# Folding a Fourier stage a second time, with padded rest rows and early small loads, in a sketched-attention and Fourier-mixing kernel

## Chip, cores and metric

One core of one Trainium2 chip at a time; kernels are compared by their ratios to the kernel before. The metric is device time in microseconds (us), median of several executions. Ratios of two kernels are computed as the mean time of one kernel's fast runs over the mean time of the other's fast runs of the same rounds, so they are not quite the ratio of the medians quoted. "State" is a label on a run: on one core a run is called slow when it lies over 1.5% above the fastest of the same kernel.

## The reference, cut to what matters

```python
# attention with quadratic sketch features, B=4, H=4, S=1088, D=32, r=8
phi(x)[i*8+j] = (S1 x)[i] * (S2 x)[j]                     # 64 features
kv = sum_s phi(k_s) v_s ;  z = sum_s phi(k_s)
x_s = phi(q_s) kv / (phi(q_s) z + 1e-6)                   # heads side by side: 128 columns
# Fourier mixing and an MLP on x [4, 1088, 128]
u  = x + real(fft(fft(x, axis=s), axis=d))
un = (u - mean) / sqrt(var + 1e-6)
out = u + relu(un @ w1) @ w2
```

The Fourier transform along s is computed as matmuls with cosine and sine tables. Because the input is real, only half of the output frequencies are computed; the other half are mirrored copies.

## The kernel before

`a` is the Fourier matmul stage for one batch and one table (i = 0 cosine, i = 1 sine). The sums x[s] + x[s+544] and x[s] - x[s+544] (even and odd frequencies) already halve the length: four chunks of 128 rows, and a rest of 64 rows, with two batches sharing one 128-row rest tile.

```python
def fold(self, t0):                      # POOL, once per half of a batch
    gpsimd.tensor_tensor(xp[:, t0:t0+2, :], xf[:, t0:t0+2, 0, :], xf[:, t0:t0+2, 1, :], ADD)
    gpsimd.tensor_tensor(xm[:, t0:t0+2, :], xf[:, t0:t0+2, 0, :], xf[:, t0:t0+2, 1, :], SUB)
    gpsimd.tensor_copy(xb[...], xf[...])         # bf16 copies of x, two
def a(self, i):
    b, tab = self.b, (ctab, stab)[i]
    r0 = 64 * (b % 2)
    bn, pz = self.pz[i] = ps(2, [[512, 2], [1, 512]])
    for par in range(2):
        xx = (xps, xms)[par][b]
        for t in range(4):
            nc.tensor.matmul(pz[:, par, 0:NK], xx[:, t, :], tab[:, t, par, :],      # NK = 273
                             start=(t == 0), stop=False)
        nc.tensor.matmul(pz[:, par, 0:NK], xrems[b // 2][r0 : r0 + 64, :],
                         tab[r0 : r0 + 64, 4, par, :], start=False, stop=True)
# ... (cut)
self.u_s = sb3.tile([128, 4, 128], FP32, name="us", tag="us")   # three buffers; stored from here
```

The program is emitted step by step from a list called ORDER, and each engine runs its own instructions in that order. The names: `wm1` a dummy matmul that wakes TensorE; `wt` transposes the sketches; `kT`, `qT` transposes of k, q on DVE; `pab` the features product of k; `tf` a step of the tables on DVE behind a POOL chain; `w1` centres the first MLP weight; `kv` the sum over k; `nd` the attention rows; `a` the Fourier stage; `us`, `st`, `mh`, `re`, `mm`, `ot` the MLP. Loads of batch 0 before: k on both queues, then the two small sketch loads, then the rest.

## Time and profile before

| | |
|---|---|
| time | 121.28 us median of 4 (120.54 to 121.82) |
| span of the profile | 119.8 us |
| first features product / first kv matmul | 11.4 / 19.4 us |
| Fourier stretch (first to last Fourier matmul) | 46.9 to 95.0 us: 48.1 us |
| after it, to the end | 24.8 us |

The three last rows are marks: the starts of the first and last matmul of a source line. They cut the span into start, middle and tail.

From the page of the kernel before: span; busy time, share and instruction count per engine; and PE busy in tenths over 40 slices of the span.

```profile
span 119.8 us, 3138 instructions
PE 105.2 (88%) x1191; PEld 70.3 (59%) x1191; DVE 79.8 (67%) x247; ACT 62.4 (52%) x148; POOL 42.0 (35%) x86
PE   6069998999999999999999999999999998966710
```

TensorE is full between the start and the tail, so work removed from it there should shorten the span until another engine takes over.

From the chain of waits of the kernel before (start, duration, what):

```profile
2.27 4.61 DMA s_68<-in_S_dram
...
7.28 4.38 PE pall L233 x10
...
47.06 0.47 PE pall L658 x4
47.52 0.22 PE pall L660
47.74 0.58 PE pall L658 x4
48.32 0.22 PE pall L660
...
103.51 3.34 DMA out_dram<-us
106.88 0.05 DVEq L558
106.97 0.70 DVE us L558
```

The sketch load is waited for and followed by ten dummies. In the Fourier stage, four full-height matmuls (L658) take 0.47 us, but the 64-row one (L660) takes 0.22 us, and the four after it take 0.58. In the tail, the chain goes through a store that is under way for 3.3 us before a copy into `us` can begin. That is not 3.3 us of idling: DVE had other work for most of it, and its waits list shows 1.2 us:

```profile
DVE us L558 <- DMA out_dram<-us: 1.2, 1, 1.2
```

From the waits of the weight loader before (line, waited for, us in total, times, longest):

```profile
PEld L660 <- issue: 3.4, 15, 0.2
```

Fifteen of the sixteen weight loads of the 64-row matmuls wait 0.23 us for nothing that the profile shows.

### The profile page before, as it was taken

The page shows a single profiled execution, that of the slowest core. Times are in us where ns is not written, and L with a number is a line of the kernel's source. Part 1 is how long each engine was busy: PE and PEld are TensorE (multiplying, and loading weights), DVE is VectorE, ACT ScalarE, POOL GpSimd, SP SyncE. Part 2 cuts the span into 40 slices and gives each one's busy share as a digit, 9 for nine tenths or more (in the row PEclk, how much of TensorE's full clock was granted, in tenths as well). Part 3 has the DMA queues.
Part 4 walks back from the last instruction along what each step waited for, and adds up shares of the span by engine and source line. Part 5 has one row for each costly group of instructions (what it writes and reads, how often), then busy time and mean ns, then how long its engine had stood idle before and what let it go on. Part 6 is the DMA issues. An engine that isn't in the chain of part 4 may idle for free.

```text
span 119.8 us, 3138 instructions
## 1 busy us (share of the span) xinstructions
PE 105.2 (88%) x1191; PEld 70.3 (59%) x1191; DVE 79.8 (67%) x247; ACT 62.4 (52%) x148; POOL 42.0 (35%) x86
## 2 busy tenths in 40 slices
PE   6069998999999999999999999999999998966710
...
GB/s 123 252 160 231 245 151 203 249 93 189 175 229 87 0 3 0 0 5 0 5 0 11 76 5 83 4 5 0 3 0 27 108 46 25 80 78 22 90 88 22
DMA packets 27967, 9.52 MB, mean 79 GB/s; under 512 B 20400, under 2 KB 26800, under 8 KB 27952
## 3 DMA queue, kind: packets, MB, share of 16 engines
...
q14 instruction: 6, 0.05, 0.1%
...
## 4 chain that ended last, share of the span: by engine, by line
PE 77%; DMA 7%; DVE 6%; ACT 3%; issue 2%; ACTq 1%; DVEq 0%
PE pall L405 13%; PE pall L493 13%; PE pall L458 8%; PE pall L331 8%; PE pall L658 7%; PE pall L614 5%; PE pall L233 4%; PE pall L595 4%; DMA s_68<-in_S_dram 4%; PE pall L660 3%; DMA out_dram<-us 3%; PE pall L680 3%; DVE stats L565 2%; DVE us L558 2%; PE pall L690 2%
## 5 line engine op out<-in xcount | busy, mean ns | idle before, releaser
L601 ACT ACTIVATE ht<-pall 128x512 bf16<-128x512 f32 (+1 forms) x36 | 18.2, 557 | 7.3 <-PE pall L595 7.2
L418 DVE TENSOR_TENSOR qpT<-pall,qa 128x1024 f32<-128x1024 f32 x8 | 9.7, 1214 | 10.7 <-PE pall L405 9.7
L614 PE MATMUL pall<-w_b,ht 128*128 128x128 bf16 x136 | 11.4, 220 | 2.0 <-ACT ht L601 0.9
L595 PE MATMUL pall<-uT,w_b 128*128 128x512 bf16 (+1 forms) x40 | 10.6, 347 | 1.8 <-ACT uT L587 1.0
L614 PEld LDWEIGHTS <-ht 128*128 128x128 bf16 x136 | 8.3, 97 | 6.4 <-ACT ht L601 2.2
L626 DVE SCALAR_TENSOR_TENSOR us<-pall,rstd,us 128x128 f32<-128x128 f32 x33 | 9.4, 345 | 1.8 <-PE pall L614 1.1
L413 ACT COPY qa<-pall 128x1024 f32<-128x1024 f32 x8 | 8.1, 1016 | 3.8 <-PE pall L405 3.6
L341 DVE TENSOR_TENSOR kp<-ka,pall 128x1024 f32<-128x1024 f32 x8 | 9.6, 1205 | 0.2 <-ACT ka L337 0.2
L331 PE MATMUL pall<-sblk,kT 128*128 128x128 f32 x64 | 9.4, 293 | 0.0
L331 PEld LDWEIGHTS pall<-sblk,kT 128*128 128x128 f32 x64 | 8.6, 206 | 0.8 <-issue 0.3
L565 DVE BATCH_NORM_STATS2 stats<-us 128x6 f32<-128x128 f32 x34 | 7.5, 280 | 1.8 <-ACT us L558 1.7
L405 PE MATMUL pall<-qT,wb 32*64 32x512 f32 x64 | 8.7, 610 | 0.0
L233 PE MATMUL pall<-wdummy 128*128 128x512 bf16 x18 | 7.5, 575 | 1.2 <-DVE wdummy L183 1.2
L405 PE MATMUL pall<-qT,wa 32*64 32x512 f32 x64 | 8.4, 606 | 0.0
L516 DVE TENSOR_TENSOR xf<-pall,rc 128x256 f32<-128x256 f32 x16 | 6.8, 425 | 0.7
L337 ACT COPY ka<-pall 128x128 f32<-128x128 f32 (+1 forms) x10 | 2.5, 249 | 8.1 <-PE pall L331 8.1
L510 DVE TENSOR_SCALAR rc<-pall 128x8 f32<-128x8 f32 (+1 forms) x20 | 3.2, 159 | 4.5 <-PE pall L493 3.4
...
L493 PEld LDWEIGHTS pall<-kvz_85,qpT 128*128 128x128 f32 x32 | 3.9, 191 | 2.5 <-issue 1.6
L558 ACT COPY us<-pall 128x512 f32<-128x512 f32 (+1 forms) x7 | 3.5, 494 | 3.2 <-PE pall L683 2.8
L298 POOL COPY cdc<-cd_192 128x128 bf16<-128x128 bf16 x1 | 0.3, 283 | 13.6 <-ACT cd_192 L296 13.6
L493 PEld LDWEIGHTS pall<-kvz_86,qpT 128*128 128x128 f32 x32 | 3.8, 192 | 1.9 <-issue 1.9
...
## 6 DMA issues: line engine op xcount, KB each, us to landing
...
```

The lines of the kernel that those rows point to most:

```text
L233: nc.tensor.matmul(w[:, :], wdummy[:, 0:128], wdummy[:, :], start=(i == 0), stop=(i == n - 1))
L331: nc.tensor.matmul(_v(self.ps, 0, 128, 32 * j, [[256, 2], [128, 2], [1, 32]]), lhsT, sblk2, start=True, stop=True, skip_group_check=True)
L341: nc.vector.tensor_tensor(out=_v(self.out, 0, 128, 0, [[64, n], [8, 8], [1, 8]]), in0=_v(self.ka, 0, 128, 0, [[8, n], [1, 8], [0, 8]]), in ...
L405: nc.tensor.matmul(pq[f0 : f0 + 64, g % 2, :], wt[32 * g : 32 * g + 32, :, :], self.qT[32 * g : 32 * g + 32, pr, 32:544], start=True, stop ...
L418: nc.vector.tensor_tensor(out=self.qpT[:, pr, :, 32:544], in0=pq, in1=self.qa[pr][:], op=MULT)
L458: nc.tensor.matmul(self.pkv[64 * h2 : 64 * h2 + 33, pr, :], lhsT, rhs, start=(j == 0 and pr == 0), stop=(j == 8), skip_group_check=True, t ...
L493: nc.tensor.matmul(pnd[:, 2 * a + pr, :], self.qpT[:, pr, a, 32 + 128 * c : 160 + 128 * c], kvz[:, pr, :], start=True, stop=True, skip_gro ...
L565: nc.vector.bn_stats(stats[:, i, :], self.u_s[:, i, :])
L595: nc.tensor.matmul(ph[:, 0:n], w1_b[:, 128 * cc : 128 * cc + 128], self.uT[:, 0:n], start=True, stop=True)
L601: nc.scalar.activation(out=self.ht[:, cc, 0:n], in_=ph[:, 0:n], func=ACT.Relu)
L614: nc.tensor.matmul(self.pm[:, i, :], self.ht[:, cc, 128 * i : 128 * i + 128], w2_b[:, cc, :], start=(cc == 0 and i == 0), stop=(cc == 3), ...
L626: nc.vector.scalar_tensor_tensor(out=ot[:, i, :], in0=self.pm[:, i, :], scalar=rstd[:, i : i + 1], in1=self.u_s[:, i, :], op0=MULT, op1=ADD)
```

## The change

The intent: x[s] and x[544-s] also share table rows up to a sign, so the folded rows can be folded once more, and two chunks do instead of four. For that, row 544-s must lie on the same partition as row s; the kernel gets it by writing half of the q feature columns reversed. The rest rows get a full 128-row tile per batch, padded with zeros. The sketch loads go first. In the same change come five buffers for `us`, a kv transpose done in two pieces, casts and reversals on other engines, 9 dummies instead of 18, and a new ORDER.

```diff
 def q_p(self, pr):
-    tensor_tensor(out=qpT[:, pr, :, 32:544], in0=pq, in1=qa, op=MULT)
+    tensor_tensor(out=qpT[:, pr, :, 32:288], in0=pq[:, :, 0:256], in1=qa[:, :, 0:256], op=MULT)
+    tensor_tensor(out=_v(qpT, 0, 128, 1088*pr + 543, [[544, 2], [-1, 256]]),
+                  in0=pq[:, :, 256:512], in1=qa[:, :, 256:512], op=MULT)
@@ fold
+def fold1(self, h, eng):      # f = x0 + x1, x0 - x1 (fp32)
+def fold2(self, h, eng):      # xc = sums and differences of the two halves of f (bf16)
@@ a
-    for t in range(4):
-        matmul(pz[:, par, 0:NK], xx[:, t, :], tab[:, t, par, :], ...)
-    matmul(pz[:, par, 0:NK], xrems[b // 2][r0:r0+64, :], tab[r0:r0+64, 4, par, :], ...)
+    combo = ((0, 3), (2, 1))[i][par]
+    for h in range(2):
+        matmul(pz[:, par, 0:NK], xcs[b][:, combo, h, :], tab[:, h, par, :], ...)
+    matmul(pz[:, par, 0:NK], xrems[b][:, :], tab[:, 2, par, :], ...)
@@ us
-    tile([128, 4, 128], FP32, name="us", tag="us")
+    tile([128, 4, 128], FP32, name="us", tag="us", bufs=5)
@@ loads of batch 0
+    the two sketch loads first on the ACT queue; q of batch 0 on the ACT queue, k head 2 on SP
 ... (cut: casts, kv transpose, reversals on DVE, ORDER)
```

More of the change, by code (lines that the diff above doesn't have):

```diff
@@ L28 @@
 ORDER = """
-wm1 wm1 wm1 wm1 wt wm1 wm1 wm1 wm1 wm1 wm1 wm1 wm1 wm1 wm1 kT0.1 wq qT0.1 qT0.0 kT0.0 pab0.1 w1 wm1
-pkr0 wm1 wm1 wm1 pab0.0 ka0.1 ka0.0 ktr0 tf0 kT1.0 kT1.1 kp0.1 tfd kp0.0 qT1.0 qA0.1 qA0.0 qB0.0
-qa0.0 qp0.0 pbr0 kv0.0 qB0.1 kar0 qa0.1 kv0.1 pab1.0 qC0 kpr0 qT1.1 qp0.1 kv0.2 ka1.0 kc0 pab1.1 kt0
-qc0 ka1.1 kz0 tf1 kp1.0 qd0 kT2.0 kp1.1 qA1.0 nd0.0 rc0.0 tf2 qa1.0 qB1.0 nd0.1 qB1.1 qA1.1 nd0.2
-qp1.0 ta1 qa1.1 tad ta0 kv1.0 kv1.1 nd0.4 nd0.3 kv1.2 pab2.0 rc0.1 qT2.1 qp1.1 rc0.2 rc0.3 fo0.1
@@ L34 @@
-fo0.0 kc1 ka2.0 kt1 kz1 qC1 ta2 qc1 qT2.0 rc0.4 kT2.1 tf3 tf4 nd1.0 qA2.1 qd1 kp2.0 rc1.0 qa2.1 ta3
-nd1.2 pab2.1 qA2.0 pkr1 qB2.1 qa2.0 ta4 qp2.1 rc1.2 nd1.1 nd1.3 a0.0 ka2.1 ktr1 z0.0 zr0.0 rc1.3
-rc1.1 kp2.1 a0.1 z0.1 zr0.1 fo1.0 fo1.1 qB2.0 kv2.0 pbr1 kv2.1 qC2 nd1.4 qp2.0 kT3.0 bb0.0 kar1
-us0.0 kpr1 rc1.4 st0.0 kv2.2 bb0.1 kc2 us0.1 st0.1 tt0.1 kt2 kz2 tt0.0 nd2.0 ut0.0 rs0.0 qc2 rc2.0
-mh0.0.0 nd2.1 mh0.0.1 mh0.0.2 re0.0.0 re0.0.2 re0.0.1 nd2.2 pab3.0 mh0.0.3 ud0.1 rc2.1 qT3.0 kT3.1
-qd2 ka3.0 re0.0.3 rs0.1 kp3.0 mh0.1.0 mm0.0.0 mm0.0.1 mm0.0.2 mm0.0.3 ot0.0 pab3.1 re0.1.0 mh0.1.3
@@ L40 @@
-mh0.1.1 re0.1.3 re0.1.1 nd2.3 rc2.2 rc2.3 qT3.1 fo2.0 mh0.1.2 qA3.0 mm0.1.0 qB3.0 mm0.1.1 re0.1.2
-qa3.0 ka3.1 mm0.1.2 mm0.1.3 qp3.0 kp3.1 ot0.1 qA3.1 a1.0 qC3 nd2.4 z1.0 qa3.1 zr1.0 a1.1 qc3 z1.1
-zr1.1 fo2.1 kv3.0 kv3.1 qB3.1 qp3.1 qd3 kv3.2 bb1.0 kc3 us1.0 tt1.0 kt3 bb1.1 kz3 st1.0 ud1.0 us1.1
-nd3.0 nd3.1 mh1.0.0 mh1.0.3 mh1.0.1 tt1.1 mh1.0.2 rc3.0 rc3.1 rc2.4 re1.0.0 re1.0.1 rs1.0 ut1.1
-re1.0.2 fo3.0 nd3.2 nd3.3 nd3.4 mm1.0.0 rc3.2 mh1.1.0 re1.0.3 re1.1.0 mh1.1.3 mh1.1.1 bbr0 re1.1.1
-rc3.3 st1.1 fo3.1 mh1.1.2 usr0 re1.1.3 re1.1.2 a2.0 mm1.0.1 mm1.1.0 mm1.1.1 mm1.1.2 mm1.1.3 ttr0
@@ L46 @@
-mm1.0.2 a2.1 mm1.0.3 rs1.1 z2.0 zr2.0 z2.1 str0 ot1.1 rc3.4 ot1.0 zr2.1 utr0 a3.0 mhr0.0 mhr0.1 a3.1
-mhr0.2 mhr0.3 z3.0 rsr0 rer0.0 z3.1 rdr0.3 rdr0.1 rer0.2 bb2.0 us2.0 st2.0 tt2.0 mmr0.0 mmr0.1
-mmr0.2 bb2.1 mmr0.3 zr3.1 zr3.0 otr0 uv2.1 st2.1 ut2.0 mh2.0.0 mh2.0.2 mh2.0.1 tt2.1 mh2.0.3 re2.0.0
-re2.0.2 re2.0.1 rs2.0 ut2.1 re2.0.3 mm2.0.0 mm2.0.1 mh2.1.0 mm2.0.2 mm2.0.3 ot2.0 mh2.1.1 mh2.1.3
-bb3.0 mh2.1.2 re2.1.0 re2.1.3 re2.1.1 rs2.1 re2.1.2 uv3.0 st3.0 mm2.1.0 mm2.1.1 bb3.1 mm2.1.2
-mm2.1.3 ot2.1 uv3.1 st3.1 tt3.0 ut3.0 mh3.0.0 re3.0.0 mh3.0.2 mh3.0.3 mh3.0.1 tt3.1 re3.0.2 re3.0.3
@@ L52 @@
-re3.0.1 rs3.0 ud3.1 mm3.0.0 mm3.0.1 mm3.0.2 mm3.0.3 mh3.1.0 bbr1 ot3.0 mh3.1.2 mh3.1.1 mh3.1.3
-re3.1.0 usr1 re3.1.1 re3.1.2 rs3.1 rd3.1.3 str1 ttr1 mm3.1.0 mm3.1.1 mm3.1.2 mm3.1.3 ot3.1 utr1 rsr1
-mhr1.0 mhr1.1 mhr1.2 mhr1.3 rer1.0 rer1.2 rdr1.1 rer1.3 mmr1.0 mmr1.1 mmr1.2 mmr1.3 obr1
+wt kT0.1 wq kT0.0 wm1 wm1 qT0.0 wm1 wm1 wm1 wm1 pab0.0 wm1 pkr0 pab0.1 qA0.0 wm1 wm1 ka0.0 ktr0
+ka0.1 w1 qT0.1 tf0 kp0.0 kp0.1 tfd kT1.0 qa0.0 qB0.0 qA0.1 pbr0 qB0.1 kv0.0 kv0.1 qa0.1 kar0 pab1.0
+qp0.0 kT1.1 kpr0 qT1.0 kv0.2 ta0 ka1.0 kc0 pab1.1 qC0 kt0 ka1.1 qc0 kz0 qp0.1 qT1.1 kp1.0 kT2.0 qd0
@@ new lines @@
+kp1.1 nd0.1 qA1.0 nd0.0 qT2.1 qa1.0 tad qB1.0 kv1.0 qA1.1 rc0.1 rc0.0 qB1.1 qp1.0 qa1.1 nd0.3 nd0.2
+kv1.1 nd0.4 pab2.0 kv1.2 tf1 qp1.1 rc0.3 fb0.1 rc0.4 rc0.2 tf2 kT2.1 qT2.0 fp0.1 fx0.1 gp0.0 fx0.0
+ta1 kc1 qC1 kt1 qA2.1 fb0.0 pkr1 ka2.0 kz1 nd1.0 pab2.1 qa2.1 qc1 ktr1 qd1 rc1.0 qB2.1 ta2 qA2.0
+qa2.0 ka2.1 qp2.1 kp2.0 nd1.1 rc1.1 nd1.2 rc1.2 kp2.1 a0.0 a0.1 pbr1 nd1.3 z0.0 rc1.3 zr0.0 fp1.1
+fx1.1 fp1.0 fx1.0 kar1 z0.1 zd0.1 qB2.0 nd1.4 kv2.0 qp2.0 kT3.1 bb0.0 qC2 kv2.1 hb1.0 hb1.1 qc2
+us0.0 kpr1 kT3.0 rc1.4 bb0.1 kv2.2 kc2 us0.1 st0.0 qd2 st0.1 tt0.1 kt2 kz2 tt0.0 nd2.0 ut0.0 mh0.0.0
@@ new lines @@
+nd2.1 rs0.1 mh0.0.2 mh0.0.1 re0.0.0 re0.0.1 re0.0.2 ut0.1 rs0.0 nd2.2 mh0.0.3 mm0.0.0 pab3.0 qT3.0
+rc2.1 rc2.0 rc2.2 qA3.0 mh0.1.0 mm0.0.1 mh0.1.1 ka3.0 re0.0.3 mh0.1.2 mm0.0.2 mm0.0.3 mh0.1.3 kp3.0
+re0.1.0 re0.1.1 qa3.0 ot0.0 pab3.1 ka3.1 re0.1.2 nd2.3 a1.0 qB3.0 mm0.1.0 mm0.1.1 re0.1.3 z1.0 kp3.1
+qT3.1 fp2.0 zr1.0 a1.1 mm0.1.2 mm0.1.3 qp3.0 ot0.1 z1.1 rc2.3 nd2.4 kv3.0 qA3.1 zr1.1 qC3 fb2.0
+qa3.1 gb2.1 qc3 rc2.4 fx2.0 fp2.1 kv3.1 qB3.1 kv3.2 qp3.1 bb1.0 kc3 kt3 fx2.1 uv1.0 tt1.0 bb1.1 kz3
@@ new lines @@
+st1.0 ut1.0 us1.1 nd3.0 tt1.1 mh1.0.0 mh1.0.1 mh1.0.3 mh1.0.2 qd3 rc3.0 st1.1 re1.0.0 re1.0.1 rs1.1
+re1.0.2 re1.0.3 ut1.1 nd3.2 nd3.4 bbr0 nd3.1 nd3.3 mm1.0.0 mm1.0.1 mh1.1.0 mh1.1.3 rc3.2 uvr0 fp3.0
+fx3.0 mh1.1.1 mh1.1.2 hb3.0 re1.1.3 rs1.0 re1.1.1 rc3.1 rc3.3 str0 re1.1.2 fp3.1 rd1.1.0 fx3.1
+mm1.0.2 a2.1 mm1.0.3 ttr0 rc3.4 a2.0 mm1.1.0 z2.0 mm1.1.1 z2.1 mm1.1.2 mm1.1.3 udr0 ot1.0 mhr0.0
+rer0.0 hb3.1 ot1.1 zd2.1 mhr0.2 a3.1 mhr0.1 a3.0 zd2.0 rdr0.2 bb2.0 mhr0.3 tt2.0 z3.1 z3.0 rsr0
+zd3.1 rdr0.3 rdr0.1 us2.0 st2.0 zd3.0 bb2.1 mmr0.0 ut2.0 mmr0.1 mh2.0.0 mmr0.2 mh2.0.3 mh2.0.2
@@ new lines @@
+mmr0.3 mh2.0.1 uv2.1 re2.0.0 otr0 st2.1 tt2.1 re2.0.2 re2.0.1 ut2.1 re2.0.3 rs2.0 mm2.0.0 mm2.0.1
+mm2.0.2 mh2.1.0 mh2.1.1 mh2.1.2 mm2.0.3 ot2.0 bb3.0 tt3.0 bb3.1 mh2.1.3 re2.1.1 re2.1.2 us3.0
+re2.1.0 ut3.0 re2.1.3 rs2.1 mm2.1.0 mh3.0.0 mm2.1.1 mm2.1.2 mh3.0.3 mm2.1.3 st3.0 uv3.1 ot2.1 st3.1
+re3.0.0 mm3.0.0 re3.0.3 mh3.0.2 bbr1 re3.0.2 mh3.0.1 re3.0.1 tt3.1 ttr1 mm3.0.1 mm3.0.2 mm3.0.3
+ut3.1 rs3.0 usr1 ot3.0 mh3.1.0 mh3.1.2 mh3.1.3 mh3.1.1 utr1 re3.1.0 re3.1.2 re3.1.1 mhr1.0 rs3.1
+rd3.1.3 mm3.1.0 mhr1.1 mm3.1.1 rer1.0 mm3.1.2 mm3.1.3 mhr1.2 mhr1.3 rer1.2 rer1.3 rer1.1 str1 rsr1
@@ L55 @@
+mmr1.0 ot3.1 mmr1.1 mmr1.2 mmr1.3 otr1
 """
@@ L145, in load @@
     def load(b):
+        if b == 0:
+            nc.scalar.dma_start(s12[0:8, :, :], _d(S1, 0, [[32, 8], [0, 4], [1, 32]]))
+            nc.scalar.dma_start(s12[8:16, :, :], _d(S2, 0, [[32, 8], [0, 4], [1, 32]]))
         for h in range(H):
-            eng = nc.scalar if (b == 0 and h >= 2) else nc.sync
+            eng = nc.scalar if (b == 0 and h == 3) else nc.sync
             eng.dma_start(
@@ L151, in load @@
             )
-        if b == 0:
-            nc.scalar.dma_start(s12[0:8, :, :], _d(S1, 0, [[32, 8], [0, 4], [1, 32]]))
-            nc.scalar.dma_start(s12[8:16, :, :], _d(S2, 0, [[32, 8], [0, 4], [1, 32]]))
-        nc.sync.dma_start(qin[b][:],
-                          _d(q, b * H * S * D, [[544, 128], [2 * S * D, 2], [1, 544]]))
+        eng = nc.scalar if b == 0 else nc.sync
+        eng.dma_start(qin[b][:],
+                      _d(q, b * H * S * D, [[544, 128], [2 * S * D, 2], [1, 544]]))
         if b % 2 == 0:
@@ L191 @@
     nc.vector.tensor_scalar(out=pcen[:], in0=ident_f[:], scalar1=1.0 / DM, scalar2=None, op0=SUB)
+    prev = const.tile([128, 128], BF16, name="prev")
+    nc.vector.tensor_copy(prev[:], _v(pdir, 0, 128, 127, [[-1, 128]]))
     bias_hpi = const.tile([128, 1], FP32, name="bias_hpi")
@@ L205 @@
         nc.gpsimd.memset(kvzs[b][:], 0.0)
-    s_f = const.tile([128, 5], FP32, name="s_f")
+    s_f = const.tile([128, 3], FP32, name="s_f")
     for g in range(4):
-        nc.gpsimd.iota(s_f[32 * g : 32 * g + 32, 0:4], pattern=[[4, 4]], base=1 + g,
+        nc.gpsimd.iota(s_f[32 * g : 32 * g + 32, 0:2], pattern=[[4, 2]], base=1 + g,
                        channel_multiplier=17, allow_small_or_imprecise_dtypes=True)
-        nc.gpsimd.iota(s_f[32 * g : 32 * g + 32, 4:5], pattern=[[1, 1]],
+        nc.gpsimd.iota(s_f[32 * g : 32 * g + 32, 2:3], pattern=[[1, 1]],
                        base=HALF * (g % 2), channel_multiplier=17,
@@ L253, in weights_q @@
         nc.vector.tensor_copy(wb[:], _v(st, 0, 128, 8, [[0, 8], [1, 8]]))
-    ctab = const.tile([128, 5, 2, NK], BF16, name="ctab")
-    stab = const.tile([128, 5, 2, NK], BF16, name="stab")
+    ctab = const.tile([128, 3, 2, NK], BF16, name="ctab")
+    stab = const.tile([128, 3, 2, NK], BF16, name="stab")
     cd2 = const.tile([128, 128], BF16, name="cd2")
@@ L274 @@
     angs = [angles(kq[:].rearrange("p a k -> p (a k)"), s_f[:, t : t + 1], 2 * NK, t)
-            for t in range(5)]
+            for t in range(3)]
     nc.gpsimd.dma_start(w2_b[:], moe_w_ch2.rearrange("(cc p) e -> p cc e", cc=4, p=128))
@@ L305, in center_w1 @@
         banks.drop(bn)
-    for t in ("d", 0, 1, 2, 3, 4):
+    for t in ("d", 0, 1, 2):
         step[f"tf{t}"] = lambda t=t: table_f(t)
@@ L312 @@
         step[f"wm{n}"] = lambda n=n: warm(n)
-    xps = [sb3.tile([128, 4, DM], BF16, name=f"xp{b}", tag="xp") for b in range(B)]
-    xms = [sb3.tile([128, 4, DM], BF16, name=f"xm{b}", tag="xm") for b in range(B)]
+    xcs = [sb3.tile([128, 4, 2, DM], BF16, name=f"xc{b}", tag="xc") for b in range(B)]
     xbs = [sb3.tile([128, 8, DM], BF16, name=f"xb{b}", tag="xb") for b in range(B)]
-    xrems = [const.tile([128, DM], BF16, name=f"xrem{i}") for i in range(B // 2)]
+    xrems = [const.tile([128, DM], BF16, name=f"xrem{b}") for b in range(B)]
+    for b in range(B):
+        nc.gpsimd.memset(xrems[b][:], 0.0)
+    kvTs = [const.tile([128, 2, 64], FP32, name=f"kvT{i}") for i in range(2)]
+    for i in range(2):
+        nc.gpsimd.memset(kvTs[i][:], 0.0)
     kprs = [const.tile([128, H, R, R], FP32, name=f"kpr{i}") for i in range(B // 2)]
@@ L370, in __init__ @@
             self.xf = sb2.tile([128, 4, 2, DM], FP32, name="xf", tag="xf")
-            self.pq, self.qa, self.pnd = {}, {}, {}
+            self.pq, self.qa, self.pnd, self.f = {}, {}, {}, {}
             for h in range(2):
@@ L376, in __init__ @@
                 step[f"pab{b}.{h}"], step[f"ka{b}.{h}"], step[f"kp{b}.{h}"] = ft.p, ft.a, ft.v
-                step[f"fo{b}.{h}"] = lambda h=h: self.fold(2 * h)
+                for (n, f, engs) in (("p", self.fold1, (nc.gpsimd, nc.vector)),
+                                     ("x", self.fold2, (nc.gpsimd, nc.vector)),
+                                     ("b", self.cast, (nc.gpsimd, nc.vector, nc.scalar))):
+                    for (e, eng) in zip("fgh", engs):
+                        step[f"{e}{n}{b}.{h}"] = lambda f=f, h=h, eng=eng: f(h, eng)
             for c in range(2):
@@ L417, in q_p @@
             bn, pq = self.pq[pr, 1]
-            nc.vector.tensor_tensor(out=self.qpT[:, pr, :, 32:544], in0=pq, in1=self.qa[pr][:],
-                                    op=MULT)
+            qa, qpT = self.qa[pr], self.qpT
+            nc.vector.tensor_tensor(out=qpT[:, pr, :, 32:288], in0=pq[:, :, 0:256],
+                                    in1=qa[:, :, 0:256], op=MULT)
+            nc.vector.tensor_tensor(out=_v(qpT, 0, 128, 1088 * pr + 543, [[544, 2], [-1, 256]]),
+                                    in0=pq[:, :, 256:512], in1=qa[:, :, 256:512], op=MULT)
             banks.drop(bn)
@@ L464, in kv_c @@
         def kv_c(self):
-            self.kvT = sb2.tile([128, 2, 64], FP32, name="kvT", tag="kvT")
+            self.kvT = kvTs[self.b % 2]
             nc.scalar.copy(self.kvT[0:33, :, :], self.pkv[0:33, :, :])
@@ L470, in kv_t @@
         def kv_t(self):
-            self.bnt, self.pt = ps(1, [[33, 2], [1, 33]])
+            self.bnt, self.pt = ps(1, [[97, 2], [1, 97]])
             for pr in range(2):
-                for h2 in range(2):
-                    r0 = 64 * h2
-                    nc.tensor.matmul(self.pt[r0 : r0 + 64, pr, :],
-                                     self.kvT[r0 : r0 + 33, pr, :],
-                                     ident_f[r0 : r0 + 33, r0 : r0 + 33],
-                                     start=True, stop=True,
-                                     skip_group_check=True, tile_position=(r0, r0))
+                nc.tensor.transpose(self.pt[0:64, pr, :], self.kvT[0:97, pr, :],
+                                    ident_f[0:97, 0:97])
         def kv_z(self):
             kvz = kvzs[self.b]
-            nc.scalar.copy(kvz[0:64, :, 0:33], self.pt[0:64, :, :])
-            nc.scalar.copy(kvz[64:128, :, 33:66], self.pt[64:128, :, :])
+            nc.scalar.copy(kvz[0:64, :, 0:33], self.pt[0:64, :, 0:33])
+            nc.scalar.copy(kvz[64:128, :, 33:66], self.pt[0:64, :, 64:97])
             banks.drop(self.bnt)
@@ L489, in nd @@
             bn, pnd = self.pnd[c] = ps(1, [[128, 4], [1, 128]])
-            for a in range(2):
-                for pr in range(2):
+            for pr in range(2):
+                for a in range(2):
                     if c < 4:
@@ L514, in x @@
             o = (_v(self.xf, 0, 128, 256 * c, [[64, 4], [32, 2], [1, 32]]) if c < 4 else
-                 _v(xrems[b // 2], p0, m, 0, [[64, 2], [32, 2], [1, 32]]))
+                 _v(xrems[b], p0, m, 0, [[64, 2], [32, 2], [1, 32]]))
             nc.vector.tensor_tensor(
@@ L519, in x, with halves, cast @@
             banks.drop(bn)
-        def fold(self, t0):
-            b, xf = self.b, self.xf
-            xp, xm, xb = xps[b], xms[b], xbs[b]
-            nc.gpsimd.tensor_tensor(out=xp[:, t0 : t0 + 2, :], in0=xf[:, t0 : t0 + 2, 0, :],
-                                    in1=xf[:, t0 : t0 + 2, 1, :], op=ADD)
-            nc.gpsimd.tensor_tensor(out=xm[:, t0 : t0 + 2, :], in0=xf[:, t0 : t0 + 2, 0, :],
-                                    in1=xf[:, t0 : t0 + 2, 1, :], op=SUB)
-            nc.gpsimd.tensor_copy(xb[:, 2 * t0 : 2 * t0 + 2, :], xf[:, t0 : t0 + 2, 0, :])
-            nc.gpsimd.tensor_copy(xb[:, 6 - 2 * t0 : 8 - 2 * t0, :], xf[:, t0 : t0 + 2, 1, :])
+        def halves(self, h):
+            return [_v(self.xf, 0, 128, 256 * h + 128 * a, [[512, 2], [1, 128]]) for a in range(2)]
+        def fold1(self, h, eng):
+            f = self.f[h] = sb2.tile([128, 2, 2, DM], FP32, name="f", tag="f")
+            x0, x1 = self.halves(h)
+            eng.tensor_tensor(out=f[:, 0, :, :], in0=x0, in1=x1, op=ADD)
+            eng.tensor_tensor(out=f[:, 1, :, :], in0=x0, in1=x1, op=SUB)
+        def fold2(self, h, eng):
+            f, xc = self.f[h], xcs[self.b]
+            eng.tensor_tensor(out=xc[:, 0:2, h, :], in0=f[:, :, 0, :], in1=f[:, :, 1, :], op=ADD)
+            eng.tensor_tensor(out=xc[:, 2:4, h, :], in0=f[:, :, 0, :], in1=f[:, :, 1, :], op=SUB)
+        def cast(self, h, eng):
+            x0, x1 = self.halves(h)
+            copy = eng.copy if eng is nc.scalar else eng.tensor_copy
+            copy(_v(xbs[self.b], 0, 128, 128 * h, [[640 - 256 * h, 2], [1, 128]]), x0)
+            copy(_v(xbs[self.b], 0, 128, 128 * (6 + h), [[-384 - 256 * h, 2], [1, 128]]), x1)
     class Mlp:
@@ L556, in us @@
         def us(self, copy=nc.scalar.copy):
-            self.u_s = sb3.tile([128, 4, 128], FP32, name="us", tag="us")
+            self.u_s = sb3.tile([128, 4, 128], FP32, name="us", tag="us", bufs=5)
             copy(self.u_s[:, 0 : self.nt, :], self.pu[:, 0 : self.nt, :])
@@ L637, in ot, with perm @@
             self.store(ot)
+    def perm(g, j):
+        return pdir[:, :, :].rearrange("p a c -> p (a c)") if g == j else prev[:, :]
     class Dft:
@@ L646, in __init__ @@
                 step[f"z{b}.{i}"] = lambda i=i: self.evac(i)
-                step[f"zr{b}.{i}"] = lambda i=i: self.rev(i)
+                step[f"zr{b}.{i}"] = lambda i=i: self.rev(i, nc.gpsimd)
+                step[f"zd{b}.{i}"] = lambda i=i: self.rev(i, nc.vector)
                 Mlp(f"{b}.{i}", 4, lambda pu, g=i: self.u(g, pu), lambda put, g=i: self.ut(g, put),
@@ L652, in a @@
             b, tab = self.b, (ctab, stab)[i]
-            r0 = 64 * (b % 2)
             bn, pz = self.pz[i] = ps(2, [[512, 2], [1, 512]])
             for par in range(2):
-                xx = (xps, xms)[par][b]
-                for t in range(4):
-                    nc.tensor.matmul(pz[:, par, 0:NK], xx[:, t, :], tab[:, t, par, :],
-                                     start=(t == 0), stop=False)
-                nc.tensor.matmul(pz[:, par, 0:NK], xrems[b // 2][r0 : r0 + 64, :],
-                                 tab[r0 : r0 + 64, 4, par, :], start=False, stop=True)
+                combo = ((0, 3), (2, 1))[i][par]
+                for h in range(2):
+                    nc.tensor.matmul(pz[:, par, 0:NK], xcs[b][:, combo, h, :], tab[:, h, par, :],
+                                     start=(h == 0), stop=False)
+                nc.tensor.matmul(pz[:, par, 0:NK], xrems[b][:, :], tab[:, 2, par, :],
+                                 start=False, stop=True)
         def evac(self, i):
@@ L669, in evac, with rev @@
             banks.drop(bn)
-        def rev(self, i):
+        def rev(self, i, eng):
             z = self.z[i]
-            nc.gpsimd.tensor_copy(z[:, 1, 0:545], _v(z, 0, 128, 544, [[-1, 545]]))
+            eng.tensor_copy(z[:, 1, 0:545], _v(z, 0, 128, 544, [[-1, 545]]))
         def u(self, g, pu):
@@ L682, in u @@
                                      skip_group_check=True)
-            nc.tensor.matmul(pu[:, :, :], pdir[:, :, :], xbs[self.b][:, 4 * g : 4 * g + 4, :],
-                             start=False, stop=True, skip_group_check=True)
+            for j in range(2):
+                nc.tensor.matmul(pu[:, 2 * j : 2 * j + 2, :], perm(g, j),
+                                 xbs[self.b][:, 4 * g + 2 * j : 4 * g + 2 * j + 2, :],
+                                 start=False, stop=(j == 1), skip_group_check=True)
         def ut(self, g, put):
@@ L695, in ut @@
                 nc.tensor.matmul(put[:, 128 * i : 128 * i + 128], xbs[self.b][:, 4 * g + i, :],
-                                 pdir[:, :, :], start=False, stop=(i == 3), skip_group_check=True)
+                                 perm(g, i // 2), start=False, stop=(i == 3),
+                                 skip_group_check=True)
         def store(self, g, ot):
@@ L712, in rest_u @@
                                  tile_position=(0, 32 * q4))
-        nc.tensor.matmul(pu[:, 0, :], ident_b[:, :], xrems[i][:, :], start=False, stop=True,
-                         skip_group_check=True)
+        for b2 in range(2):
+            nc.tensor.matmul(pu[:, 0, :], ident_b[:, :], xrems[2 * i + b2][:, :], start=False,
+                             stop=(b2 == 1), skip_group_check=True)
     def rest_ut(i, zz, put):
```

2 lines of the change are left out of this document (1 added, 1 removed).

## The prediction

> **What bounds the kernel now.** TensorE. The page gives PE 105.2 us busy of a 119.8 us span (88%), DVE 67%, ACT 52%; the chain of waits is 77% PE. In the busy times by stretch PE is full from 7 to 97 us. The exceptions: the start (PE waits 4.0 us for the sketch load, then runs ten dummy matmuls until 11.7 us) and the tail (24.5 us remain after the last Fourier matmul at 95.3; PE is busy 2.9 of 5 us in 105-110, and the chain holds 3.3 us in which a copy into "us" waits for an output store to free its buffer). DVE is nearly full in 16-25 us.
>
> **Terms.**
>
> 1. Fourier stage, PE. On the chain its four batches take 3.07, 3.17, 2.97 and 2.98 us: 12.2 us for 80 matmuls of 273 columns. Full-height ones run at 0.117 us; a 64-row rest matmul takes 0.22 us, and PEld idles 0.23 us before each. After: 48 full-height ones, my estimate 48 x 0.117 = 5.6 us. (The Trainium skill, "TensorE: Matmul & The Clock Gate", Back-to-back issue gap: N/2.4 + 2.5 = 116 ns; the trace agrees.) Saved 6.6 us, nearly all on the chain.
> 2. Transpose of the kv state: 0.35 us x4 becomes two transposes each (one took 0.11 us on the chain): saves 0.7 us. Extra rest and permutation matmuls cost 0.3 us.
> 3. Start. Sketch weights appear at about 3.3 us, not 7.0; half the dummies go. Real PE work starts near 7 us, not 11.4, then waits for loads (rest rows of k near 9.6 us, w1 near 10; 230 GB/s in the slices). The first features product still waits behind a table step whose POOL input is ready at 12.9 us. First kv matmul near 16.5 us, not 19.4: saves about 3 us. Risk: dummies ran at 0.43 us until 13 us, 0.22 after; the same page, Part 1, wants about 3.4 us of sustained work for full speed, and a gappy PE may get it only at 13-16 us, costing 1-2 us.
> 4. Tail. Five "us" buffers remove the 3.3 us wait; ACT (relu 0.6 us each) and DVE (1.7 us statistics, 1.4 us output a group) then set the pace: saves about 2 us.
> 5. Other engines. Two tables fewer: ACT -4.1, DVE -1.4 us. More: second fold on POOL (about 2.9 us per half, not 2.3), casts to ACT (about 3 us), five reversals and some folds on DVE, qp split in two (8 x 0.1 us). DVE stays near 82 us, above 85% in the middle: I charge 1.5 us of new PE waits.
>
> **Sum.** -6.6 - 0.4 - 3 - 2 + 1.5 = -10.5 us: span 109.3; the time was 1.5 us above the span: **110.8 us**, range **107.5 to 115.0**. Chances: faster by over 2% **0.95**, within 2% **0.04**, slower **0.01**.
>
> **What would show it.** 48 Fourier matmuls, 1.4 us a batch on the chain, no idle weight loads before the rest ones (1). First kv matmul at 16-17.5 us (3). No store in the middle of the chain (4). PE busy near 94 us. New PE waits on DVE or POOL of 1 to 3 us in all (5).
>
> **What would make it wrong.** Cold clock beyond 16 us; the two-level fold on POOL, about 3 us behind the last attention row, holding back a Fourier stage (likeliest batches 2 and 3); reversed accesses on DVE much slower than forward ones; the tail bound by ACT and DVE, so that nothing of term 4 and only part of term 1 for the last batches is kept.

## The result

The changed kernel took 111.63 us median of 4 (110.98 to 112.37); ratio 0.921, 95% interval 0.913 to 0.929. The span of the profile is 109.2 us where 109.3 was predicted.

| mark (us) | before | after | moved |
|---|---|---|---|
| first kv matmul | 19.4 | 17.7 | -1.7 |
| first Fourier matmul | 46.9 | 43.8 | -3.1 |
| Fourier stretch, length | 48.1 | 42.8 | -5.3 |
| from its end to the end | 24.8 | 22.5 | -2.3 |
| span | 119.8 | 109.2 | -10.6 |

The page after, the same lines:

```profile
span 109.2 us, 3042 instructions
PE 93.8 (86%) x1138; PEld 66.6 (61%) x1138; DVE 82.2 (75%) x263; ACT 60.8 (56%) x149; POOL 43.0 (39%) x87
PE   0469879989999899999999999999997899999400
```

PE lost 11.4 us of busy time. The chain of waits of this profile stops after two pieces (0.4 us), so it cannot be set beside the one of before; marks, timelines and stretches stand in for it.

The Fourier stage of the first batch after, in the timeline of PE (start, duration from first to last of the row, what; L681 folded, L683 rest):

```profile
43.84 0.40 PE L681 MATMUL pall<-ctab,xc_216 128*128 128x273 bf16 x2
44.08 0.28 PE L683 MATMUL pall<-ctab,xrem_224 128*128 128x273 bf16 x1
44.19 0.40 PE L681 MATMUL pall<-ctab,xc_216 128*128 128x273 bf16 x2
44.42 0.28 PE L683 MATMUL pall<-ctab,xrem_224 128*128 128x273 bf16 x1
44.54 0.40 PE L681 MATMUL pall<-stab,xc_216 128*128 128x273 bf16 x2
...
45.24 0.39 PE L339 MATMUL pall<-sblk,kTr 128*128 128x128 f32 x2
```

Twelve matmuls from 43.84 to 45.24: 1.40 us, where the stage took about 3.05 us before, and a rest matmul now starts as evenly as the others (0.24 us after two). The wait of PEld before the rest weights is gone.

The stretch has other waits instead. Before, PE was busy in all of its 48.1 us; after, it is busy in 41.9 of 42.8 us and stands idle for 0.9 us at two places:

```profile
83.15 0.39 PE L681 MATMUL pall<-ctab,xc_218 128*128 128x273 bf16 x2 [0.62 <-DVE ht L627]
85.33 0.39 PE L681 MATMUL pall<-stab,xc_219 128*128 128x273 bf16 x2 [0.31 <-ACT z_263 L691]
```

PE waits there for a relu of the MLP on DVE (`ht`), and for ACT to copy out the result of an earlier Fourier stage (`z`).

The start after, in the timeline of PE (the bracket is the idle time before, and what ended it):

```profile
4.20 0.26 PE L249 MATMUL pall<-ident_f,s_68 16*128 16x16 f32 x1 [4.20 <-DMA s_68<-in_S_dram]
4.38 2.74 PE L237 MATMUL pall<-wdummy 128*128 128x512 bf16 x6
8.28 1.16 PE L339 MATMUL pall<-sblk,kT 128*128 128x128 f32 x8 [1.16 <-DVE kT L405]
...
12.58 1.13 PE L307 MATMUL pall<-w_f,pcen 128*128 128x512 f32 x2 [0.31 <-DMA w_f<-in_moe_w_ch_dram]
14.38 1.09 PE L417 MATMUL pall<-qT,wb 32*64 32x512 f32 x8 [0.68 <-ACT w_b L308]
```

The weights are there at 4.2 us instead of 7.0, and the first features product runs at 8.3 instead of 11.4. Then PE stands behind w1. From DVE's waits:

```profile
DVE tx_203 L286 <- POOL tr_204 L273: 4.0, 1, 4.0
DVE kT L405 <- DMA kin_76<-in_k_dram: 2.9, 1, 2.9
```

DVE waits 4.0 us for the table step before it may work on the features, and later 2.9 us for k of batch 2. The 3 us that TensorE is ahead at 8.3 us are down to 1.7 us at the first kv matmul.

The end, in the timelines of the SP queue: the last two rows of the kernel after, then those of before. They are the stores' issues.

```profile
93.41 11.73 SPq L727 DMA_DIRECT2D out_dram<-us  x16
105.25 1.92 SPq L757 DMA_DIRECT2D out_dram<-us  x4
```

```profile
101.58 14.21 SPq L701 DMA_DIRECT2D out_dram<-us  x16
115.89 1.93 SPq L729 DMA_DIRECT2D out_dram<-us  x4
```

After, the last arithmetic (DVE) ends at 103.93 us, but the last four stores start to be issued only at 105.25, because SP is still issuing those of the group before. Before, the last arithmetic ended at 115.39 and the issue began at 115.89. So 5.3 us follow the last arithmetic, against 4.4 before: the compute got shorter than the row of stores behind it.

### The profile page after: what moved, and what is told of

The parts are those of the page before. It is cut to its first block, busy times and chain, and to the rows that moved or that the text cites. A ratio compares the mean times of both kernels' runs of the same rounds, so it can differ in the third digit from the quotient of the medians.

```text
span 109.2 us, 3042 instructions
## 1 busy us (share of the span) xinstructions
PE 93.8 (86%) x1138; PEld 66.6 (61%) x1138; DVE 82.2 (75%) x263; ACT 60.8 (56%) x149; POOL 43.0 (39%) x87
## 5 line engine op out<-in xcount | busy, mean ns | idle before, releaser
L634 PEld LDWEIGHTS <-ht 128*128 128x128 bf16 x136 | 8.9, 98 | 4.6 <-ACT ht L621 2.3
L537 POOL TENSOR_TENSOR f<-xf 128x256 f32<-128x256 f32 x7 | 5.1, 733 | 12.7 <-DVE xf L526 12.7
L339 PE MATMUL pall<-sblk,kT 128*128 128x128 f32 x64 | 8.9, 282 | 1.2 <-DVE kT L405 1.2
L339 PEld LDWEIGHTS pall<-sblk,kT 128*128 128x128 f32 x64 | 7.9, 192 | 2.4 <-DVE kT L405 2.1
L431 DVE TENSOR_TENSOR qpT<-pall,qa 128x512 f32<-128x512 f32 x8 | 5.4, 679 | 2.5 <-PE pall L417 2.5
L433 DVE TENSOR_TENSOR qpT<-pall,qa 128x512 f32<-128x512 f32 x8 | 5.4, 679 | 0.0
L607 ACT CAST uT<-pall 128x512 bf16<-128x512 f32 (+1 forms) x9 | 5.0, 554 | 0.7 <-PE pall L720 0.4
L503 PEld LDWEIGHTS pall<-kvz_85,qpT 128*128 128x128 f32 x32 | 3.8, 191 | 2.4 <-issue 1.6
L538 POOL TENSOR_TENSOR f<-xf 128x256 f32<-128x256 f32 x7 | 5.1, 723 | 0.0
L615 PEld LDWEIGHTS <-w_b 128*128 128x128 bf16 x40 | 3.6, 98 | 2.1 <-issue 0.8
L503 PE MATMUL pall<-kvz_85,qpT 128*128 128x128 f32 x32 | 4.4, 285 | 0.5 <-ACT kvz_85 L494 0.5
```

The costliest lines, as they stand in the source:

```text
L339: nc.tensor.matmul(_v(self.ps, 0, 128, 32 * j, [[256, 2], [128, 2], [1, 32]]), lhsT, sblk2, start=True, stop=True, skip_group_check=True)
L431: nc.vector.tensor_tensor(out=qpT[:, pr, :, 32:288], in0=pq[:, :, 0:256], in1=qa[:, :, 0:256], op=MULT)
L503: nc.tensor.matmul(pnd[:, 2 * a + pr, :], self.qpT[:, pr, a, 32 + 128 * c : 160 + 128 * c], kvz[:, pr, :], start=True, stop=True, skip_gro ...
L615: nc.tensor.matmul(ph[:, 0:n], w1_b[:, 128 * cc : 128 * cc + 128], self.uT[:, 0:n], start=True, stop=True)
L634: nc.tensor.matmul(self.pm[:, i, :], self.ht[:, cc, 128 * i : 128 * i + 128], w2_b[:, cc, :], start=(cc == 0 and i == 0), stop=(cc == 3), ...
```

## The experiments

Twelve kernels, five rounds each; all were correct. Two theories were up: **A**, that TensorE binds the middle, so the padding and the halved number of matmuls are worth their PE time; and rivals B, C and F, that the gain is elsewhere or partly absorbed. Theory D and rivals E, G, H are about the start and the tail.

### 1. Undoing the parts of the Fourier stage: c_after, e_nopad, e_zeromm, e_bothundone

c_after is the changed kernel as it is. e_nopad:

```diff
-    matmul(pz[:, par, 0:NK], xrems[b][:, :], tab[:, 2, par, :], start=False, stop=True)
+    r0 = 64 * (b % 2)
+    matmul(pz[:, par, 0:NK], xrems[b][r0:r0+64, :], tab[r0:r0+64, 2, par, :], start=False, stop=True)
```

e_zeromm gives the 32 matmuls back without touching the folds (wdummy holds zeros):

```diff
     for h in range(2):
         matmul(pz[:, par, 0:NK], xcs[b][:, combo, h, :], tab[:, h, par, :], ...)
+    for h in range(2):
+        matmul(pz[:, par, 0:NK], wdummy[:, 0:128], tab[:, h, par, :], start=False, stop=False)
```

e_bothundone has both edits. Expected:

> The changed kernel unedited, as the base for the others of this call. Both theories: 111.6 us, within 1 us.

> The changed kernel with the padding of the rest rows undone in the Fourier stage alone: its 16 rest matmuls are 64 rows high again (same result). Theory A (the middle is bound by TensorE, and a 64-row matmul costs about 0.295 us with its two shape changes instead of 0.117, from 3.05 us a batch before less 16 x 0.117, over 4): +2.8 us over c_after, and PEld idles 0.23 us before each rest matmul. Rival B (the gain is the new order and the start; the middle is now paced by DVE or POOL): under +1 us. Rival C (the gain of the Fourier stage is only the halved number of matmuls; padding gives nothing): 0 us here.

> The changed kernel with the 32 removed full-height Fourier matmuls given back as matmuls by zero weights (same result, same folds on POOL and DVE). Theory A: 32 x 0.117 = +3.7 us over c_after. Rival B: under +1 us. Rival C: +6.6 us.

> Both edits together: the Fourier stage has the 80 matmuls and the 16 low ones of before. Theory A: +6.6 us over c_after, the two add up (118.2 us), and the Fourier stage takes about 3.05 us a batch. Rival B: under +2 us.

Measured (median, ratio to before; then the Fourier stretch of the one profile each):

| run | us | ratio | over c_after, by ratio | Fourier stretch |
|---|---|---|---|---|
| c_after | 112.39 | 0.919 | | 42.8 |
| e_nopad | 113.46 | 0.932 | +1.5 | 45.5 |
| e_zeromm | 114.17 | 0.935 | +2.0 | 46.1 |
| e_bothundone | 117.83 | 0.970 | +6.1 | 48.9 |

The fourth column is the difference of the ratios times 121.84 us. The profiles of c_after and e_nopad are of runs labelled slow. Without them: the stretch is 42.8 in the profile of after, 46.1 in e_zeromm and 48.9 in e_bothundone, so the matmuls are worth 3.3 us in the stretch and the padding 2.8 on top. Both together cost 6.1 us end to end, close to the predicted 6.6: B and C fall. Within the stretch, from after to e_bothundone, PE's busy time grows by 6.8 us (41.9 to 48.7), and its idle time falls from 0.9 to 0.2 us.

The weight loader's waits in e_bothundone:

```profile
PEld L687 <- issue: 3.6, 16, 0.2
```

All sixteen waits of 0.23 us are back as soon as the rows are 64 high. The Trainium skill says under "TensorEngine Tiling (Array Packing)", Key Properties, that changing the tiling mode drains the TensorE. This trace agrees as far as it goes: it shows the waits, 3.6 us in all and none with padded rows, but not that a drain is their reason.

A did not fully hold either: each edit alone cost only 1.5 to 2 us end to end, though the stretch grew by about 3. Either noise had eaten the rest, or there was slack outside the stretch. The start marks hinted at noise: the first kv matmul came at 17.5 us in e_zeromm and at 19.0 in e_bothundone, with the same instructions up to there.

### 2. Two starts of the same kernel: i_warm, w_nopad, w_zeromm

From the timelines of PE at the start, e_bothundone (compare with the profile of after above, rows at 8.28 us):

```profile
4.31 2.74 PE L237 MATMUL pall<-wdummy 128*128 128x512 bf16 x6
8.29 2.07 PE L339 MATMUL pall<-sblk,kT 128*128 128x128 f32 x8 [1.24 <-DVE qT L410]
10.16 0.63 PE L237 MATMUL pall<-wdummy 128*128 128x512 bf16 x1
...
18.96 1.26 PE L473 MATMUL pall<-kp,vin 128*33 128x64 f32 x38
```

The same features product takes 2.07 us here and 1.16 us in the profile of after. TensorE was still at half pace, although the profile's granted clock says 1.00 in these stretches of both. i_warm fills the time in which PE waits for the sketches:

```diff
-wt kT0.1 wq kT0.0 wm1 wm1 qT0.0 ...
+wm1 wm1 wm1 wm1 wm1 wm1 wm1 wt kT0.1 wq kT0.0 wm1 wm1 qT0.0 ...
```

w_nopad and w_zeromm are e_nopad and e_zeromm with the same seven dummies. Expected:

> The changed kernel with seven dummy matmuls put ahead of the sketch transpose, where TensorE waits idle from 1.2 to 4.2 us. The profiles so far show two starts of the changed kernel: TensorE at full speed by 8.3 us (first features product 1.16 us, first kv matmul at 17.5 to 17.7) or slow until about 13 us (the same product 2.08 us, first kv at 19.0 to 19.6). Theory D (which start comes is a matter of how long TensorE has worked without a gap): always the fast start, first kv at 17.7 or below, median 110.8 to 111.2, the runs within 1 us of each other. Rival E (the spread is the loads, the dummies change nothing): median 112 with a spread of 2 us, both starts still seen.

> i_warm with the padding of the rest rows undone in the Fourier stage, to repeat e_nopad without the lottery of the start. Theory A, if the 1.1 to 1.4 us seen before was only that noise: +2.7 us over i_warm, as the stretch from the first to the last Fourier matmul had grown (42.9 to 45.5). Rival F (half of it is absorbed by slack elsewhere): +1.4 us.

> i_warm with the 32 Fourier matmuls given back with zero weights. Theory A: +3.3 us over i_warm, as the stretch had grown (42.9 to 46.1). Rival F: +1.9 us.

Measured: i_warm 111.73 us, ratio 0.917, six runs from 111.29 to 112.10. Its profile:

```profile
4.51 2.26 PE L211 MATMUL pall<-wdummy 128*128 128x512 bf16 x6
8.31 1.16 PE L313 MATMUL pall<-sblk,kT 128*128 128x128 f32 x8 [1.53 <-DVE kT L379]
...
17.38 1.98 PE L447 MATMUL pall<-kp,vin 128*33 128x64 f32 x64
```

The features product took 1.16 us, the fast start, in the profiles of five of the six kernels with the leading dummies (i_warm, w_nopad, w_zeromm, w_us3, i_all); the sixth, i_all2, is taken up below. The spread fell from 2.25 us (c_after) to 0.81 us, but w_nopad and w_zeromm, with the same dummies, spread by 1.88 and 1.93 us, so a smaller spread is not shown. The median is above the 110.8 to 111.2 that D had set. So D holds, five times of six, for the start alone, and its size was too hopeful: over all six runs each, fast and slow, i_warm's mean over before's is 0.915 and c_after's is 0.922, under 1% better and within the intervals of the two.

One half of E falls: the dummies do change something. The row of six dummies behind the sketch transpose took 1.72 to 2.60 us in all six profiles with the leading dummies, and 2.74 us in all six without them (after, c_after, e_nopad, e_zeromm, e_bothundone, e_loads), so the full speed does come earlier. The other half stands: the loads spread the time too. In the slow profile of w_nopad, which has the fast start, DVE waits 3.7 us for k of batch 2, where i_warm waits 2.8, and the first Fourier matmul comes at 44.5 us instead of 43.7.

The sixth profile shows what the dummies do not secure. Stretches of i_all2 (us, length, busy time of PE, PEld, DVE, ACT, POOL, then PEclk, DMA share, GB/s):

```profile
8.00:10.00 2.00, 1.70 (x9) 1.64 (x10) 1.22 (x5) 1.28 (x1) 1.91 (x4) 0.65 1.43 161
10.00:12.00 2.00, 2.00 (x10) 1.80 (x9) 1.22 (x1) 0.53 (x2) 1.82 (x5) 0.50 1.01 232
12.00:14.00 2.00, 2.00 (x19) 0.78 (x21) 1.35 (x2) 0.87 (x2) 1.83 (x4) 0.99 1.07 204
```

Here TensorE had reached full speed early (its second row of six dummies took 1.79 us instead of 2.74), then stood idle for 2.0 us (6.31 to 8.30) while k was transposed, and was set back to half speed until about 12 us. The features product took 1.81 us. In this profile the column PEclk does show it; the cold start of e_bothundone, before the first rise, it shows as 1.00.

The Trainium skill, "TensorE: Matmul & The Clock Gate", Part 1, describes just this: full speed comes after about 3.4 us of sustained work as a free-running window sees it, so the same kernel can warm up at different points. The runs agree as far as they go: 2.74 us of dummies with a gap behind them were sometimes enough and sometimes not.

The repeats did not rescue A's sum:

| run | us | ratio | over i_warm, by ratio | Fourier stretch |
|---|---|---|---|---|
| i_warm | 111.73 | 0.917 | | 42.8 |
| w_nopad | 113.35 | 0.930 | +1.5 | 45.5 (slow run) |
| w_zeromm | 113.66 | 0.933 | +1.9 | 46.1 |

Rival F had the end-to-end numbers right twice. Yet the stretch grew by 2.7 and 3.3 us again, so whatever gives half of it back lies outside it. Between the profiles of i_warm and w_zeromm the start was 0.8 us shorter (Fourier start 43.7 and 42.9) and the tail 0.6 us shorter (23.5 and 22.9). The start can be read: the first kv matmul comes at 17.4 us in both, and after it DVE waits 2.8 us for a load of k in i_warm and 1.6 us for a load in w_zeromm. That is where loads land, and not the edit, which acts only later. The tails lie between 22.4 and 23.5 us in all profiles of this order with five buffers and the stores on SP, so one profile each cannot say more. The intervals of the ratios, about 0.005 or 0.6 us to each side, leave room for part of the gap, though it came up twice. Its cause remains open; what is shown is that undoing either part alone costs 1.5 to 2 us, and both 6.

### 3. The padding alone, in the kernel before: b_pad

Four zeroed rest tiles, one per batch, full-height rest matmuls, one more matmul in each of the four rest steps (the text below says two); everything else as before.

```diff
-xrems = [const.tile([128, DM], BF16) for i in range(B // 2)]
+xrems = [const.tile([128, DM], BF16) for b in range(B)]      # and a memset of each
-    matmul(pz[:, par, 0:NK], xrems[b // 2][r0:r0+64, :], tab[r0:r0+64, 4, par, :], ...)
+    matmul(pz[:, par, 0:NK], xrems[b][:, :], tab[:, 4, par, :], ...)
```

> The kernel before with the padding of the rest rows alone (four zeroed full-height rest tiles, two more matmuls in each rest step). Theory A (TensorE bound): the Fourier stretch shrinks from 48.1 to 45.4 us, 2.4 to 2.8 us faster than before, ratio 0.978. Rival F (about half of such a gain is absorbed outside the stretch, as undoing it gave 1.5 of 2.7 us): ratio 0.987.

Measured: 119.40 us, ratio 0.976, interval 0.970 to 0.982: 2.9 us faster. The stretch went from 48.1 to 45.3 us (profile of a slow run). In both stretches PE is never idle, and there A is right in full: sixteen matmuls given more rows, and no more useful work, bring 2.4%. The record calls this "unclear" because the interval reaches across the 2% line; it lies well clear of no change. The profile itself shows only part of the gain (span 118.4 us), since in that run the Fourier stretch began 1.5 us later than in the profile of before.

### 4. The early sketch loads: e_loads

```diff
-    if b == 0: the two sketch loads first; k head 3 and q on the ACT queue
+    k heads 2 and 3 on the ACT queue, then the two sketch loads; q on SP        # as before
```

> The changed kernel with the loads of batch 0 issued as before (sketches behind k, q on the other queue). Theory A (the early sketches are what the start gains, term 3 of the prediction): sketch transpose at 7.0 us, dummies cold until 9.6, first kv matmul at 20 us instead of 17.5 to 19.6, +2.5 us over the changed kernel (111.7 to 112.4). Rival G (the start is held by the table step, by w1 and by the loads of batch 2 anyway): at most +1 us, Fourier start at 44 to 45.5 us as in the runs of the changed kernel.

Measured: 112.83 us, ratio 0.925, so 0.5 us over the changed kernel by the ratio first measured (0.921) and 0.8 by that of c_after. G holds. The profile, timeline of PE and the same DVE step as above:

```profile
7.04 2.74 PE L236 MATMUL pall<-wdummy 128*128 128x512 bf16 x6
9.57 1.91 PE L338 MATMUL pall<-sblk,kT 128*128 128x128 f32 x8
```

```profile
13.64 2.35 DVE L348 TENSOR_TENSOR kp<-ka,pall 128x1024 f32<-128x1024 f32 x2
```

The intervals of e_loads (0.920 to 0.931) and c_after (0.912 to 0.926) overlap, so even this much is not certain. The sketches are 2.7 us later, PE is slow and its first product 1.3 us later, and still DVE starts on the features at 13.64 us, against 13.62 in the profile of after and 13.63 in that of c_after, since both stand behind the same table step on POOL. The first kv matmul is late, at 19.8 us, but there is no wait for k of batch 2 any more: being early had only turned into that wait.

### 5. Five buffers for us: w_us3

```diff
-    tile([128, 4, 128], FP32, name="us", tag="us", bufs=5)
+    tile([128, 4, 128], FP32, name="us", tag="us")                # three; on top of i_warm
```

> i_warm with three buffers for the tile us instead of five (term 4). Theory A: the copy of a late group waits 2 to 3 us for a store again, +2 us over i_warm, and the stretch after the last Fourier matmul grows from 22.5-23.5 to 25 us. Rival H (the new order alone had removed that wait): 0 us.

Measured: 117.89 us, ratio 0.967: 6.0 us over i_warm, three times what A had. The stretch after the last Fourier matmul grew from 23.5 to 29.6 us, while start and Fourier stretch stayed (43.6 and 42.8). The waits in the tail of w_us3:

```profile
ACT us L552 <- DMA out_dram<-us: 3.7, 1, 3.7
DVE stats L559 <- ACT us L552: 3.2, 3, 1.4
DVE us L552 <- DMA out_dram<-us: 2.4, 2, 1.6
```

6.1 us of waiting for stores, where the kernel before has 1.2 us of it on DVE. H falls, and so does the picture of the buffers as a small fix. The new order lets the groups of the last two batches follow each other so closely that with three buffers the tail would be longer than the old one's 24.8 us.

### 6. A version that beats both: i_all, i_all2

i_all adds three moves in ORDER to i_warm and sends the last rest stores from the ACT queue; i_all2 splits the last eight stores evenly.

```diff
 ORDER (i_all)
-  qA0.0 wm1 wm1 ka0.0 ktr0 ka0.1 w1 qT0.1 tf0 kp0.0 kp0.1 ... qB0.1 kv0.0 ... kp1.0 kT2.0 qd0 kp1.1
+  qA0.0 ka0.0 ktr0 ka0.1 qT0.1 kp0.0 kp0.1 tf0 ... qB0.1 w1 kv0.0 ... kp1.0 qd0 kp1.1 kT2.0
 rest_store
-  nc.sync.dma_start(...)
+  (nc.scalar if i == 1 else nc.sync).dma_start(...)               # i_all
+  (nc.scalar if i == 1 and b2 == 1 else nc.sync).dma_start(...)   # i_all2
 store (i_all2)
-  nc.sync.dma_start(...)
+  (nc.scalar if self.b == 3 and g == 1 and i >= 2 else nc.sync).dma_start(...)
```

> A version meant to beat both: i_warm, and the first features product no longer behind the table step on DVE, the w1 product moved behind the third q product, the third batch's k transpose moved behind kp of the second, and the last rest stores issued from the ACT queue. If the start is held by these waits: first kv at about 15 us (-2.5), Fourier start about 2 us earlier. If the loads hold it instead: Fourier start unchanged within 0.5 us, and a wait on the loads of batch 1 or 2 in place of those. The stores: the end comes 4 us after the last DVE instruction instead of 5.3 (-1.3 us). Together 107.5 to 109 us if both hold, 109.7 if only the stores do.

> i_all with the last eight stores split evenly: two of the last group and two of the rest on the ACT queue, the others on SP. In i_all the last SP store issue of the group ends 105.2 us, 2.6 us after the last matmul. If the issue of stores (0.55 us each, one after the other) ends the kernel: another -0.7 us against i_all (ratio 0.9005 to 0.895). If the landing of the stores does: unchanged.

Measured: i_all 109.89 us, ratio 0.9005; i_all2 109.54 us, ratio 0.897, interval 0.891 to 0.902. i_all2 is about 2.4% faster than the changed kernel (0.897 over 0.919).

The start hardly gained (and the profiled run of i_all2 had the slow start shown above). In i_all the features are formed from 9.8 us on instead of 13.6, but the first kv matmul came only at 16.7 us and the Fourier start moved from 43.7 to 43.4. DVE's waits there:

```profile
DVE kT L379 <- DMA kin<-in_k_dram: 3.5, 2, 1.9
DVE qT L384 <- DMA qin<-in_q_dram: 1.0, 1, 1.0
```

With the waits on the table and on w1 gone, DVE waits 4.5 us for loads of k and q instead: the second branch of what was expected. The tail did gain, from 23.5 us (i_warm) to 21.8 and 21.3. The last issues of i_all2, SP queue and ACT queue:

```profile
93.49 11.24 SPq L701 DMA_DIRECT2D out_dram<-us  x14
104.84 1.02 SPq L731 DMA_DIRECT2D out_dram<-us  x2
```

```profile
103.14 1.32 ACTq L701 DMA_DIRECT2D out_dram<-us  x2
104.58 0.99 ACTq L731 DMA_DIRECT2D out_dram<-us  x2
```

The last arithmetic ends at 103.88 us, and the kernel ends 4.0 us later, not 5.3. In i_all, with the four rest stores alone on the ACT queue, it ends 4.5 us later, where 4 had been expected. The split of i_all2 alone is worth 0.0036 in the ratio, 0.4 us of the 0.7 expected, and less than the intervals of the two.

## Why the prediction was right, point by point

The time and the sum were right (110.8 predicted, 111.63 measured; span 109.3 and 109.2). The terms:

1. **Fourier stage, -6.6 us: right.** Undoing both parts cost 6.1 us by ratio: 6.8 us of PE work in the stretch, less 0.7 us of waits that came in its place. Against before, the stretch shrank by only 5.3 us, mainly because the new order also moved one attention row product, nd1.3, of about 0.9 us from before the stretch into it. With both parts undone the stretch is 48.9 us, 0.8 longer than the 48.1 before. That each part alone is worth so much less end to end was not foreseen, and its cause is open.
2. **Kv transpose, -0.7, extras +0.3: small, not run alone.** The piece went from 0.35 us to 0.26 us (36.75 to 37.01 in the profile of after), so about 0.4 us for four.
3. **Start, -3 us: right in size by luck, wrong in its reason.** The Fourier start moved by 3.1 us in the profile of after, of which about 0.9 is the moved nd1.3, and by only 1.8 us in that of c_after, with the slow start. The first kv matmul, predicted at 16 to 17.5 us, came at 17.7 and 19.6 us in these two, and the early sketches are worth 0.5 to 0.8 us, not 3. What the new order and the fewer dummies give at the start was not run alone. The prediction had named the table step and w1 as waits, but not the loads of batch 2, which take back what was ahead. The cold clock that it listed as a risk is real in some runs and not in others, and with it the gap of TensorE between the dummies and the first transposed k.
4. **Tail, -2 us: right in size (-2.3), mis-sized in its part.** The prediction had the buffers remove a 3.3 us wait, read off the chain; DVE had idled for 1.2 us of it. Under the new order they remove 6 us of waiting, so the buffers and the order are one step and cannot be priced apart. The tail also gave back 0.9 us at the very end, where SP's issue of stores became the last thing running.
5. **New waits, +1.5 us: about right in size, partly wrong in place.** In the stretch PE waits 0.9 us (0.6 for DVE, 0.3 for ACT), where the kernel before has none. Between the first kv matmul and the stretch it waits 0.9 us more for ACT's copies of the kv state before and after its transposes, which it did not before. None of it is for the two-level fold on POOL, the risk that was named, and 1.2 of the 1.8 us are for ACT, which was not. DVE's busy time was as expected (82.2 us). The reversed writes cost no more than forward ones: 0.68 us for the reversed half, 0.69 for the forward one, though the two together take 0.15 us more than the single operation of before (1.21 us).

So the total owes something to luck: the early sketches gave far less than the 3 us set down for the start, the moved nd1.3 and probably the new order made up for it, and the profile that was taken happens to have the fast start.

## What to carry to other kernels

Where TensorE is full, look for its silent costs: a matmul of other height among full ones costs its own time and a delay on both sides (0.22 us instead of 0.12, and 0.58 for the next four instead of 0.47), and zero padding to full height took 2.4% off a kernel without removing any work. Being early at the start is worth only what the next load allows, so follow the gain to the next wait before counting it. When compute in the tail gets denser, the buffers that stores drain from, and the one queue that issues the stores, must grow with it.

## What the Trainium skill lacked or had wrong

- "TensorE: Matmul & The Clock Gate", the table "Why this matters for your kernels", says that one K=32 matmul takes the same time as K=128. The records here agree for 64 rows by themselves (0.288 against 0.280 us each), but among full-height ones they cost far more: b_pad, which only pads sixteen of them, is 2.9 us faster, 0.18 us each. The page on tiling names the drain but gives no time for it; here PEld idles 0.23 us before each.
- The same page, Part 1, says that the clock falls after an idle window of about 3.4 us. In i_all2 it fell although TensorE was wholly idle for only 2.0 us. The column PEclk reads 1.00 up to 8.5 us, 0.62 in the half microsecond after and 0.50 from 9 us on, so the fall came near 8.6 us; of the 3.4 us before it, TensorE was idle for about 60%, by our estimate from these numbers. If the page's window holds, a mostly idle one was enough here. In w_nopad 1.7 us of idling left the features product at its fast 1.16 us.
- The same page, Part 1, puts the cost of the warm-up at under 1% of a typical span and advises not to fit it. For the mean that holds (0.922 against 0.915), and it says that the number of slow matmuls varies with the phase of the window, but not what that is worth in a kernel whose start is part of the critical path: here the first kv matmul came at 17.7 or 19.6 us in two profiles of one kernel (features product 1.16 or 2.08 us), and the Fourier start at 43.8 or 45.1. Its warning that the recorded clock events can't be trusted fits: the granted clock reads 1.00 in both starts of the changed kernel's order, the slow one included.
- "DMA: Bandwidth & Descriptors", Issuing engines are not separate DMA queues, says that issuing from several engines saves only issue time, usually small against the transfer. At this kernel's end it was not small: about 0.5 us per store one after the other (1.92 us for the last four), and moving four of the last eight stores to a second queue cut the time after the last arithmetic from 5.3 to 4.5 us (i_all) and 4.0 us (i_all2).
- No page gives a measured time for a reversed access pattern. Here a DVE multiply of 128x512 fp32 with a reversed output took 0.68 us, the forward one 0.69, and a reversed bf16 copy of 128x545 took 0.30 us on DVE against 0.64 us on POOL.
